# Batch two's v in natural layout through DRAM, and another use of the load buffers

## The chip, the cores and the metric

One core of one Trainium2 chip. The metric is the device time of one execution in microseconds (us). The kernel before takes 226.39 us (median; 226.32 to 226.49). The profile has a span of 224.3 us, since the time also holds some 2 us around it.

## The reference, cut to what matters

```python
batch, n_heads, seq, head_dim = (4, 8, 768, 64);  n_blocks = 8
# P (8 x 8 per head) from sort_net: five rounds of exp and row/column normalisation
k_sorted = einsum('bhij,bhjcd->bhicd', P, k_b)      # blocks of k mixed by P
v_sorted = einsum('bhij,bhjcd->bhicd', P, v_b)      # the same for v
attn = softmax(scale * q_b @ k_sorted^T)            # inside each block of 96
x = attn @ v_sorted                                 # -> (3072 tokens, 512)
h = max(x @ w_in, 0);  out = (h * h) @ w_out        # 512 -> 2048 -> 512
```

## The kernel before

A planner in the kernel lays all work in one order: the attention of one batch fills TensorE between the matrix products of the feed-forward part of the batch before. It fixes the order on TensorE, ScalarE, VectorE and SyncE.

Batches one and two sort v by 128-row matmuls into `vsT`, and turn it by TensorE transposes into `vs`. Batches three and four do it on 32x32 tiles in natural layout, and re-tile the result by a write to DRAM and a read back:

```python
# batches one and two: sort, then turn
for a in range(NA):
    for h in range(2):
        nc.tensor.matmul(out=tp[64*h:64*(h+1), a, :], lhsT=src[:, 2*u.hp+h, D*a:D*(a+1)],
                         rhs=w_all[...], start=True, stop=True)
...
    nc.tensor.transpose(out=vbp[:, n, :], in_=u.vsT[...], identity=ident)

# batches three and four (s_nat): two pairs of heads, 16 matmuls each
nc.tensor.matmul(out=p2[slot][32*c:32*(c+1), h, 0:NA*D], lhsT=w_t[r, ...], rhs=src[r, g, ...],
                 tile_position=(r.start, 32*c))
...
nc.sync.dma_start(out=v_way[b, g]..., in_=vn_r[m]...)     # write
nc.sync.dma_start(out=vb_r[w]..., in_=v_way[b, g]...)     # read back in blocks
```

The attention output of batch two, pairs 0 to 2, goes into `xT` by DMA transposes on SyncE's queue; the feed-forward part of batch two cannot start before all of it is there:

```python
def s_xt(u, due=0, eng=AD):
    if u.b > 1 or u.b == 1 and u.hp < HP - 1:
        def turn(e):
            nc.sync.dma_start_transpose(out=xT[:, u.hp, S*u.b:S*(u.b+1)]..., in_=u.ao...)
```

Loads have two buffers each for q, k and v (`bufs=2`), so batch three takes the first batch's and batch four the second's:

```python
qkv[b] = [ld.tile([128, H, NA * D], BF16, tag=t, name=t) for t in ("qb", "kb", "vb")]
...
def load_late(b):
    for g in range(2):              # first four heads, then last four
        for t in (1, 2, 0):         # k, v, q
            load(b, t, HP * g, HP)
```

The softmax here doesn't subtract the row's maximum and nothing guards it: scores larger than these inputs give would overflow.

Of the kernel before, what the change touches and what calls it, by code (L numbers as in the profile page):

```python
# [128 lines left out]
def kernel(  # L129
# [10 lines left out]
    nc = tc.nc  # L140
# [75 lines left out]

    ksT_r, vsT_r, et_r, vs_r = [], [], [], []
    for n in range(3):
        for r, name, hs in ((ksT_r, "ksT", 2), (vsT_r, "vsT", 2)):
            sT = const.tile([128, hs, HS + 32], BF16, name=f"{name}{n}")  # L220
            nc.vector.memset(sT[:, :, HS:HS + 32], 0.0)
            r.append(sT)
        vs = const.tile([96, NB, 2, 66], BF16, name=f"vs{n}")
        nc.vector.memset(vs[:, :, :, D:D + 1], 1.0)
        vs_r.append(vs)
# [32 lines left out]
    def dma(key, mb, dst_src, deps=()):  # L258
        def issue(e):
            dst, src = dst_src()  # L260
            nc.gpsimd.dma_start(out=dst, in_=src)  # L261
        op = plan.add("POOL", 0.75, issue, deps)
        landed[key] = plan.add("DMA", mb / 0.39, lambda e: None, [op, landed.get("last")])
        landed["last"] = landed[key]

    readers = {b: [] for b in range(B)}

    def alloc_qkv(b):
        if b not in qkv:
            qkv[b] = [ld.tile([128, H, NA * D], BF16, tag=t, name=t) for t in ("qb", "kb", "vb")]  # L270

    def load(b, t, h0, n, p=slice(0, 128)):
        def dst_src():
            alloc_qkv(b)
            if b > 1 and t:
                return (qkv[b][t].rearrange("p (g h) x -> p g (h x)", h=HP)[:, h0 // HP, :],
                        kv_t[t][b, :, h0 // HP, :])
            return qkv[b][t][p, h0:h0 + n, :], (q_r, k_r, v_r)[t][b, p, h0:h0 + n, :]
        dma((b, t, h0, p.start), 1.57 * n / H * (p.stop - p.start) / 128, dst_src,
            readers[b - 2] + [x_done[b - 1, x, 0] for x in range(HP)] if b > 1 else [])  # L280

    def load_w_in(g):
        f = slice(d_ff // 4 * g, d_ff // 4 * (g + 1))
# [7 lines left out]
    mask = const.tile([128, C0], BF16)  # L291
    mask_t = const.tile([128, 4], BF16)

    def make_mask(e):

        src, w = ident, 64
        while w >= 4:
            dst = {C0: mask, 4: mask_t}.get(w) or const.tile([128, w], BF16, name=f"fold{w}")
            nc.gpsimd.tensor_tensor(out=dst, in0=src[:, 0:w], in1=src[:, w:2 * w], op=ALU.add)
            src, w = dst, w // 2  # L300

    for g in range(HP):
        load(0, 1, 2 * g, 2)
# [3 lines left out]
    load_w_in(0)  # L307
    for g in range(1, 4):
        load_w_in(g)
    for g in range(4):  # L310
        t = slice(NT // 4 * g, NT // 4 * (g + 1))
        dma(("w_out", g), 1.05, lambda t=t: (w_out_bf[:, t, :], w_out_r[:, t, :]))
    for g in range(2):
        for t in (2, 1, 0):
            load(1, t, HP * g, HP)


    rs = const.tile([NH, NB], FP32)
# [69 lines left out]
    def build_w(h0, n, src, dep):  # L388
        def fn(e):
            s = tiles["pt_01"] if src is None else src  # L390
            nc.vector.tensor_tensor(
                out=w_all[:, h0:h0 + n, :, :],
                in0=mask[:, None, None, :].to_broadcast([128, n, NB, C0]),
                in1=s[:, :, h0:h0 + n].rearrange("p i h -> p h i")[:, :, :, None]
                .to_broadcast([128, n, NB, C0]),
                op=ALU.mult)
        op = plan.add("DVE", 0.15 + 0.134 * n, fn, [dep])
        for h in range(h0, h0 + n):
            built[h] = op
        return op  # L400
# [94 lines left out]
    def s_sort(u, t, due=0, early=False, eng=AD):  # L495

        st = {}

        def mm(e):
            src = qkv[u.b][t]  # L500
            if early:
                tp = psf.tile([128, 512], FP32, tag="pf", name="tp")
                tp = tp[:, 0:NA * u.ni * C0].rearrange("p (a x) -> p a x", a=NA)
            else:
                tp = (p2[s2].rearrange("p b x -> p (b x)")[:, 0:NA * u.ni * C0]
                      .rearrange("p (a x) -> p a x", a=NA))
            st["p"] = tp
            for a in range(NA):
                for h in range(2):
                    nc.tensor.matmul(  # L510
                        out=tp[64 * h:64 * (h + 1), a, :],
                        lhsT=src[:, 2 * u.hp + h, D * a:D * (a + 1)],
                        rhs=w_all[:, H * u.b + 2 * u.hp + h, u.i0:u.i0 + u.ni, :]
                        .rearrange("p i c -> p (i c)"),
                        start=True, stop=True)

        def ev(e):
            h0 = u.halves[0]
            copy(e, (u.ksT if t == 1 else u.vsT)[:, h0:h0 + len(u.halves), 0:HS]
                 .rearrange("p h (x a) -> p h x a", a=NA),  # L520
                 st["p"].rearrange("p a (h x) -> p h x a", x=NQ * C0))

        h0 = 2 * u.hp
        dep = landed[u.b, t, h0 if u.b == 0 else HP * (h0 // HP), 0]
        ring = rf if early else r2
        s2, old = ring.take()
        pe = plan.add("PE", 0.336 if u.full else 0.2, mm,
                      [dep, built[H * u.b + h0], built[H * u.b + h0 + 1]] + old, due, mode="col")
        readers[u.b].append(pe)
        op = one_of(eng, cost_f(NA * C0 * u.ni), ev, [pe] + u.old)  # L530
        ring.use(s2, pe, op)
        return op

    def s_sc(u, due=0):
# [3 lines left out]
        for hf in u.halves:  # L538
# [4 lines left out]
            def mm(e, hf=hf, st=st, slot=slot):  # L543
# [4 lines left out]
                for n in range(NQ):  # L548
                    for h in range(2):
                        nc.tensor.matmul(  # L550
                            out=scp[:, h, BLK * n:BLK * (n + 1)],
                            lhsT=(u.ksT[64 * h:64 * (h + 1), hf, BLK * n:BLK * n + 128]
                                  if u.b < 2 else
                                  kx_r[u.kx][64 * h:64 * (h + 1), NQ * hf + n::NB]),
                            rhs=(qT[64 * h:64 * (h + 1), NQ * hf + n, :] if u.b < 2 else
                                 qT[64 * h:64 * (h + 1), :, C0 * (NQ * hf + n):
                                    C0 * (NQ * hf + n + 1)]),
                            start=True, stop=True)
# [31 lines left out]
    def s_vt(u, due=0, eng=AD):  # L590
# [3 lines left out]
        def mm(e):  # L594
            st["p"] = vbp = ps1.tile([128, u.ni, 128], BF16, tag="p1", name="vbp")
            for n in range(u.ni):
                i = u.i0 + n
                nc.tensor.transpose(  # L598
                    out=vbp[:, n, :],
                    in_=u.vsT[:, i // NQ, BLK * (i % NQ):BLK * (i % NQ) + 128],  # L600
                    identity=ident)

        def ev(e):
# [13 lines left out]
    def s_nat(b, g, t, due):  # L617
# [4 lines left out]
        for hp in (2 * g, 2 * g + 1):  # L622
# [3 lines left out]

            def mm(e, hp=hp, slot=slot):
                src = qkv[b][t].rearrange("p (g h) x -> p g (h x)", h=HP)
                for h in range(2):
                    r = slice(32 * (2 * (hp % 2) + h), 32 * (2 * (hp % 2) + h + 1))  # L630
                    for c in range(4):
                        nc.tensor.matmul(  # L632
                            out=p2[slot][32 * c:32 * (c + 1), h, 0:NA * D],
                            lhsT=w_t[r, HP // 2 * b + g, :, :].rearrange("p c i -> p (c i)"),
                            rhs=src[r, g, NA * D * c:NA * D * (c + 1)],
                            start=True, stop=True, tile_position=(r.start, 32 * c))

# [25 lines left out]
                out=vb_r[w].rearrange("p i h x -> p (i h x)"),  # L663
                in_=v_way[b, g].rearrange("a (c i) x -> (a c) (i x)", i=NB))

        wr = plan.add("SP", 0.33, write, evs + [loaded(b)])
        there = plan.add("WAY", 2.0, lambda e: None, [wr])
        rd = plan.add("SP", 0.33, read, [there] + oldw)
        back = plan.add("WAY", 2.0, lambda e: None, [rd])
        rvn.use(m, *evs, there)  # L670
        rvb.use(w, back)
        v_blk[b, g] = w, back

    def loaded(b):
        return [landed[b, t, HP, 0] for t in (0,)][0]

    def s_turn(b, hp):

# [35 lines left out]

    def s_av(u, due=0):
        nao, olda = rao.take()
        if u.b > 1:
            w, u.vs_op = v_blk[u.b, u.hp // 2]
        u.norms = []
        for hf in u.halves:  # L720
# [4 lines left out]
            def mm(e, hf=hf, st=st, slot=slot):  # L725
# [3 lines left out]
                for n in range(NQ):  # L729
                    for h in range(2):  # L730
                        nc.tensor.matmul(  # L731
                            out=oup[:, h, 66 * n:66 * n + D + 1],
                            lhsT=et_r[u.et[hf]][:, h, BLK * n:BLK * n + 128],
                            rhs=(u.vs[:, NQ * hf + n, h, 0:D + 1] if u.b < 2 else
                                 vb_r[w][:, NQ * hf + n, 2 * (u.hp % 2) + h, 0:D + 1]),
                            start=True, stop=True)

# [13 lines left out]
            op = plan.add("DVE", 0.9, norm, [pe])  # L751
            r2.use(s2, pe, op)
            ret.use(u.et[hf], pe)
            if u.b < 2:
                rks.use(u.n, pe)
            else:
                rvb.use(w, pe)
# [179 lines left out]
    def lay(b, halves, c0, c1):  # L937
        step, gap = (c1 - c0) / (HP + 0.9), (c1 - c0 - 13) / (HP - 1)
        for hp in range(HP):
# [3 lines left out]
            def open_(due, b=b, hp=hp, box=box):  # L943
# [2 lines left out]
                if b == 1:  # L946
                    build_w(H * b + 2 * hp, 2, pt, kops[b - 1, hp])
                u.k_op = kops[b, hp] = s_sort(u, 1, due)
                u.v_op = s_sort(u, 2, due)

            for f, s in ((0.0, open_),
                         (0.35, lambda due, box=box: s_sc(box["u"], due)),
                         (0.5, lambda due, box=box: s_vt(box["u"], due)),
                         (0.75, lambda due, box=box: s_av(box["u"], due)),
                         (1.2, lambda due, box=box: s_xt(box["u"], due))):
                todo.append((c + step * f, len(todo), s, b))
# [1 line left out]
    def lay_late(b, c0):  # L958

        todo.append((c0, len(todo), lambda due: load_late(b), 0))  # L960
        if b == 2:
            todo.append((c0, len(todo), build_wt, 0))
        for g in range(2):
            for t in (1, 2):
                todo.append((c0 + 9 + 9 * g, len(todo),
# [12 lines left out]
            todo.append((c + 3, len(todo), lambda due, box=box: s_xt(box["u"], due), b))  # L978

    def load_late(b):  # L980
        for g in range(2):
            for t in (1, 2, 0):
                load(b, t, HP * g, HP)

    lay(0, (1,), 0, n_up)
    lay(1, (0, 1), n_up, 2 * n_up)
    lay_late(2, 2 * n_up)
    lay_late(3, 4 * n_up)
    for due, _, stage, b in sorted(todo, key=lambda x: x[:2]):
        stage(int(due))  # L990
# [43 lines left out]
```

## Time and profile before

| | before |
|---|---|
| time, span | 226.39 us, 224.3 us |
| TensorE busy | 97% of the span |
| TensorE waits after 22 us | none listed |
| feed-forward of batch two begins | 82.6 us |
| batch two's DMA transposes of xT | issued from 56.5 to 70.5 us, landing 3.0 to 7.1 us later |

In the time views, a line is start, length, engine, source line, operation, output<-input, shapes and count; a bracket gives the idle time before it and what ended it. In the list of waits, the numbers are us in total, times, and the longest. "To landing" is the time from a transfer's issue to its last byte. Of the names, `p` is a product in PSUM (the memory that TensorE writes to), `hp` and `op` are the up- and the down-projection's, `ao` is the attention output and `xT` the same turned, `kn` the sorted k and `kx` the same turned; an eviction is the copy of a product out of PSUM by VectorE or ScalarE. The prediction below shows the views of the kernel before on which it rests.

### The profile page before, as it was taken

What the parts mean: (1) busy time and instruction counts of PE and PEld (TensorE: products, weight loads), DVE (VectorE), ACT (ScalarE), POOL (GpSimd) and SP (SyncE); (2) the same over time, 40 slices, a digit from 0 to 9 for tenths busy, and PEclk for the clock granted to TensorE, in tenths of its full rate; (3) what the DMA queues carried; (4) which work ended last, traced back from release to release, by engine and by line L of the source; (5) the groups of instructions that cost most, each with busy time, mean ns of one, the idle gap of its engine ahead of it and who ended that gap; (6) DMA issues with size and microseconds to landing.
All of it is one profiled execution on the core that took longest, in us unless ns stands there. A gap on an engine that the chain in (4) does not pass through costs nothing.

```text
span 224.3 us, 5245 instructions
## 1 busy us (share of the span) xinstructions
PE 216.6 (97%) x2130; PEld 122.9 (55%) x2145; DVE 105.7 (47%) x297; ACT 122.1 (54%) x253; POOL 26.4 (12%) x46
## 2 busy tenths in 40 slices
PE   7898999999999999999999999999999999999994
PEld 2476665556665645545665455445665465446553
DVE  6777777317666416640666127523664045005400
ACT  4665776228885328734775248535774177137521
POOL 7962332200004200000000000000000000000000
PEclk9999999999999999999999999999999999999999
DMA  5999999999953996499941320899522410110012
GB/s 66 201 202 208 207 206 205 203 227 245 210 65 27 191 239 145 115 216 201 220 38 35 85 94 0 164 225 254 110 37 43 122 47 1 50 57 37 0 50 94
DMA packets 42744, 28.83 MB, mean 129 GB/s; under 512 B 22752, under 2 KB 38368, under 8 KB 42720
## 3 DMA queue, kind: packets, MB, share of 16 engines
q0 software_dynamic: 13888, 13.63, 37.1%
q1 hardware_dynamic: 28832, 14.86, 29.7%
q8 instruction: 17, 0.28, 0.5%
q14 instruction: 7, 0.06, 0.1%
HBM read 28.89 MB, written 7.91 MB: 164 GB/s over the span
## 4 chain that ended last, share of the span: by engine, by line
PE 92%; DMA 2%; DVE 2%; ACT 1%; issue 1%; ACTq 0%; POOLq 0%
PE hp L810 37%; PE op L838 35%; PE p L550 4%; PE p L731 3%; DMA qb<-in_q_dram 2%; PE p L510 2%; PE qtp L461 2%; PE vbp L598 2%; PE op L872 2%; PE p L350 1%; PE p L632 1%; PE xtp L779 1%; PE tp L510 1%; DVE ao L742 1%; ACT h L818 0%
## 5 line engine op out<-in xcount | busy, mean ns | idle before, releaser
L810 PE MATMUL hp<-xT,w_in_bf 128*128 128x384 bf16 x512 | 91.0, 326 | 0.0
L838 PE MATMUL op<-w_out_bf,h 128*128 128x512 bf16 x353 | 82.6, 379 | 0.8
L818 ACT ACTIVATE h<-hp 128x384 bf16<-128x384 f32 x128 | 62.0, 495 | 23.5 <-PE hp L810 20.0
L821 DVE TENSOR_TENSOR h<-h 128x384 bf16<-128x384 bf16 x128 | 44.5, 355 | 56.3 <-ACT h L818 55.5
L810 PEld LDWEIGHTS <-w_in_bf 128*128 128x128 bf16 x512 | 47.0, 98 | 30.0 <-issue 0.7
L838 PEld LDWEIGHTS <-h 128*128 128x128 bf16 x368 | 34.7, 98 | 39.4 <-issue 0.7
L192 ACT COPY ob<-op 128x512 f32<-128x512 f32 (+1 forms) x25 | 14.2, 569 | 56.0 <-PE op L838 50.6
L742 DVE TENSOR_TENSOR ao<-p,rec 96x512 bf16<-96x512 f32 x32 | 22.0, 687 | 1.4 <-DVE rec L741 0.3
L582 ACT ACTIVATE et<-p 96x384 bf16<-96x384 f32 x48 | 19.4, 491 | 2.4 <-PE p L550 2.4
L741 DVE RECIPROCAL rec<-p 96x8 f32<-96x8 f32 x32 | 6.4, 199 | 13.6 <-PE p L731 13.3
L731 PEld LDWEIGHTS <-et 96*128 96x128 bf16 x256 | 10.6, 97 | 2.9
L261 POOL DMA_DIRECT2D qb<-in_q_dram x8 | 6.0, 754 | 32.5 <-PE qtp L461 24.4
L350 PE MATMUL p<-ones 128*128 128x512 bf16 (+1 forms) x36 | 8.8, 360 | 1.1 <-DVE ones L213 1.1
L194 DVE COPY vs<-vbp 96x512 bf16<-96x512 bf16 (+1 forms) x12 | 6.1, 508 | 7.1 <-PE vbp L598 6.9
L573 ACT ACTIVATE et<-p 96x768 bf16<-96x768 f32 x8 | 6.3, 802 | 2.1 <-PE p L550 2.0
L261 POOL DMA_DIRECT2D kb<-in_k_dram x10 | 6.6, 659 | 6.6 <-DMA w_in_bf<-in_moe_w_in_dram 2.2
L261 POOL DMA_DIRECT2D vb<-in_v_dram x10 | 6.6, 660 | 6.4 <-DMA w_in_bf<-in_moe_w_in_dram 3.6
L192 ACT CAST ksT<-p 128x768 bf16<-128x768 f32 (+1 forms) x7 | 4.6, 662 | 3.3 <-PE p L510 3.3
L550 PEld LDWEIGHTS <-kx 64*128 64x128 bf16 x128 | 4.6, 155 | 2.8 <-issue 2.8
L731 PE MATMUL p<-vs,et 96*128 96x65 bf16 x128 | 6.0, 193 | 0.0
L461 PE MATMUL qtp<-ident,qb 64*64 64x64 bf16 (+1 forms) x144 | 4.7, 204 | 1.3 <-DMA qb<-in_q_dram 1.3
L461 PEld LDWEIGHTS <-qb 64*64 64x64 bf16 (+1 forms) x144 | 3.5, 109 | 4.5 <-DMA qb<-in_q_dram 2.3
(78 smaller groups left out, 129.3 us busy)
## 6 DMA issues: line engine op xcount, KB each, us to landing
out_dram<-ob SPq DMA_DIRECT2D x23, 256.0 KB, 2.8
qb<-in_q_dram POOLq DMA_DIRECT2D x8, 384.0 KB, 15.7
vb<-in_v_dram POOLq DMA_DIRECT2D x6, 384.0 KB, 17.1
kb<-in_k_dram POOLq DMA_DIRECT2D x6, 384.0 KB, 17.1
w_in_bf<-in_moe_w_in_dram POOLq DMA_DIRECT2D x4, 512.0 KB, 12.5
w_out_bf<-in_moe_w_out_dram POOLq DMA_DIRECT2D x4, 512.0 KB, 18.0
v_way<-vn SPq DMA_DIRECT2D x4, 396.0 KB, 4.1
vblk<-v_way SPq DMA_DIRECT2D x4, 396.0 KB, 3.9
```

The costliest lines, as they stand in the source:

```text
L192: nc.scalar.copy(out=out, in_=in_)
L261: nc.gpsimd.dma_start(out=dst, in_=src)
L350: nc.tensor.matmul(out=out, lhsT=ones, rhs=rhs, start=True, stop=True)
L461: nc.tensor.transpose(out=t["p"][64 * h:64 * (h + 1), a, :], in_=qb[p0:p1, 2 * hp + h, D * a:D * (a + 1)], identity=ident[p0:p1, p0:p1])
L550: nc.tensor.matmul(out=scp[:, h, BLK * n:BLK * (n + 1)], lhsT=(u.ksT[64 * h:64 * (h + 1), hf, BLK * n:BLK * n + 128] if u.b < 2 else kx_r[ ...
L582: nc.scalar.activation(out=et[:, h, 0:HS].rearrange("p (n c a) -> p n c a", c=C0, a=NA), in_=st["p"][0:96, h, 0:HS].rearrange("p (n a c) - ...
L731: nc.tensor.matmul(out=oup[:, h, 66 * n:66 * n + D + 1], lhsT=et_r[u.et[hf]][:, h, BLK * n:BLK * n + 128], rhs=(u.vs[:, NQ * hf + n, h, 0: ...
L742: nc.vector.tensor_tensor(out=u.ao[:, n0:n0 + NQ, :, :].rearrange("p n e d -> p e n d"), in0=ov[:, :, :, 0:D], in1=rec[:, :, :, None].to_b ...
L810: nc.tensor.matmul(out=t["hp", nt][:, 0:HS], lhsT=w_in_bf[:, kc, 128 * nt:128 * (nt + 1)], rhs=xT[:, kc, t0:t0 + HS], start=(kc == 0), sto ...
L818: nc.scalar.activation(out=t["h1", nt], in_=t["hp", nt][:, 0:HS], func=AF.Relu)
L821: nc.vector.tensor_tensor(out=t["h2"][:, nt, :], in0=t["h1", nt], in1=t["h1", nt], op=ALU.mult)
L838: nc.tensor.matmul(out=t["op", mt], lhsT=t["h2"][:, nt, 128 * mt:128 * (mt + 1)], rhs=w_out_bf[:, nt, :], start=(nt == 0), stop=(nt == NT ...
```

## The change

Batch two's v goes the way that batches three and four go: 32 matmuls on 32x32 tiles in place of 48 sorting matmuls and 32 transposes on TensorE, and four transfers through DRAM more. Half of that v is loaded ahead of w_out. Batch three takes the second batch's buffers, batch four the first's, and late loads take the last four heads first. The cuts leave out a second mask for batch two's order of k, the flat `ksT` and `vsT`, new estimates of transfer times and a new `loaded` in the planner (the load behind which late work is planned), and renamed indices.

```diff
 def alloc_qkv(b):
     if b not in qkv:
-        qkv[b] = [ld.tile([128, H, NA * D], BF16, tag=t, name=t) for t in ("qb", "kb", "vb")]
+        m = (b + 1) // 2 % 2
+        qkv[b] = [ld.tile([128, H, NA * D], BF16, tag=f"{t}{m}", name=t, bufs=1)
+                  for t in ("qb", "kb", "vb")]
...
-            readers[b - 2] + [x_done[b - 1, x, 0] for x in range(HP)] if b > 1 else [])
+            readers[(0, 0, 1, 0)[b]] + [x_done[b - 1, x, 0] for x in range(HP)] if b > 1 else [])
...
+    load(1, 2, 0, HP)                 # ahead of w_out
...
-    for g in range(2):
-        for t in (2, 1, 0):
-            load(1, t, HP * g, HP)
+    for t, g in ((2, 1), (1, 0), (0, 0), (1, 1), (0, 1)):
+        load(1, t, HP * g, HP)
...
-                u.v_op = s_sort(u, 2, due)
+                if b == 0:
+                    u.v_op = s_sort(u, 2, due)
+            if b == 1 and hp % 2 == 0:
+                todo.append((14 + 2 * hp, len(todo),
+                             lambda due, g=hp // 2: s_nat(1, g, 2, due), b))
...
-        for g in range(2):
+        for g in (1, 0):
             for t in (1, 2, 0):
                 load(b, t, HP * g, HP)
...
+    todo.append((8, len(todo), build_wt, 0))
-    lay_late(2, 2 * n_up)
+    lay_late(2, 2 * n_up + 3)
```

More of the change, by code (lines that the diff above doesn't have):

```diff
@@ L218 @@
     for n in range(3):
-        for r, name, hs in ((ksT_r, "ksT", 2), (vsT_r, "vsT", 2)):
-            sT = const.tile([128, hs, HS + 32], BF16, name=f"{name}{n}")
-            nc.vector.memset(sT[:, :, HS:HS + 32], 0.0)
+        for r, name in ((ksT_r, "ksT"), (vsT_r, "vsT")):
+            sT = const.tile([128, S + 32], BF16, name=f"{name}{n}")
+            for x in (HS, S):
+                nc.vector.memset(sT[:, x:x + 32], 0.0)
             r.append(sT)
@@ L262, in dma @@
         op = plan.add("POOL", 0.75, issue, deps)
-        landed[key] = plan.add("DMA", mb / 0.39, lambda e: None, [op, landed.get("last")])
+        landed[key] = plan.add("DMA", mb / (0.39 if key[0] == 0 else 0.43), lambda e: None, [op, landed.get("last")])
         landed["last"] = landed[key]
@@ L274, in dst_src @@
             alloc_qkv(b)
-            if b > 1 and t:
+            if b > 1 and t or b == 1 and t == 2:
                 return (qkv[b][t].rearrange("p (g h) x -> p g (h x)", h=HP)[:, h0 // HP, :],
@@ L292 @@
     mask_t = const.tile([128, 4], BF16)
+    mask_1 = const.tile([128, C0], BF16)
     def make_mask(e):
@@ L300, in make_mask @@
             src, w = dst, w // 2
+        nc.gpsimd.tensor_copy(out=mask_1.rearrange("p (z y) -> p z y", y=4),
+                              in_=mask.rearrange("p (y z) -> p z y", z=4))
     for g in range(HP):
@@ L392, in fn @@
                 out=w_all[:, h0:h0 + n, :, :],
-                in0=mask[:, None, None, :].to_broadcast([128, n, NB, C0]),
+                in0=(mask if h0 < H else mask_1)[:, None, None, :]
+                .to_broadcast([128, n, NB, C0]),
                 in1=s[:, :, h0:h0 + n].rearrange("p i h -> p h i")[:, :, :, None]
@@ L517, in ev @@
         def ev(e):
-            h0 = u.halves[0]
-            copy(e, (u.ksT if t == 1 else u.vsT)[:, h0:h0 + len(u.halves), 0:HS]
-                 .rearrange("p h (x a) -> p h x a", a=NA),
-                 st["p"].rearrange("p a (h x) -> p h x a", x=NQ * C0))
+            dst = u.ksT if t == 1 else u.vsT
+            if u.b == 0:
+                copy(e, dst[:, BLK * u.i0:BLK * (u.i0 + u.ni)]
+                     .rearrange("p (x a) -> p x a", a=NA), st["p"].rearrange("p a x -> p x a"))
+            else:
+                copy(e, dst[:, 0:S].rearrange("p (n a x) -> p n a x", a=NA, x=C0),
+                     st["p"].rearrange("p a (n x) -> p n a x", x=C0))
         h0 = 2 * u.hp
@@ L551, in mm @@
                             out=scp[:, h, BLK * n:BLK * (n + 1)],
-                            lhsT=(u.ksT[64 * h:64 * (h + 1), hf, BLK * n:BLK * n + 128]
+                            lhsT=(u.ksT[64 * h:64 * (h + 1), HS * hf + BLK * n:HS * hf + BLK * n + 128]
                                   if u.b < 2 else
@@ L599, in mm @@
                     out=vbp[:, n, :],
-                    in_=u.vsT[:, i // NQ, BLK * (i % NQ):BLK * (i % NQ) + 128],
+                    in_=u.vsT[:, BLK * i:BLK * i + 128],
                     identity=ident)
@@ L628, in mm @@
                 src = qkv[b][t].rearrange("p (g h) x -> p g (h x)", h=HP)
+                w = w_t[:, HP // 2 * b + g, :, :].rearrange("p c i -> p (c i)")
                 for h in range(2):
@@ L633, in mm @@
                             out=p2[slot][32 * c:32 * (c + 1), h, 0:NA * D],
-                            lhsT=w_t[r, HP // 2 * b + g, :, :].rearrange("p c i -> p (c i)"),
+                            lhsT=w[r, :],
                             rhs=src[r, g, NA * D * c:NA * D * (c + 1)],
@@ L664, in read @@
                 in_=v_way[b, g].rearrange("a (c i) x -> (a c) (i x)", i=NB))
-        wr = plan.add("SP", 0.33, write, evs + [loaded(b)])
-        there = plan.add("WAY", 2.0, lambda e: None, [wr])
+        wr = plan.add("SP", 0.33, write, evs + ([loaded(b)] if b > 1 else []))
+        slow = 6.0 if b == 1 else 2.0
+        there = plan.add("WAY", slow, lambda e: None, [wr])
         rd = plan.add("SP", 0.33, read, [there] + oldw)
-        back = plan.add("WAY", 2.0, lambda e: None, [rd])
+        back = plan.add("WAY", slow, lambda e: None, [rd])
         rvn.use(m, *evs, there)
@@ L674, in loaded @@
     def loaded(b):
-        return [landed[b, t, HP, 0] for t in (0,)][0]
+        return landed[b, 0, 0, 0]
     def s_turn(b, hp):
@@ L716, in s_av @@
         nao, olda = rao.take()
-        if u.b > 1:
+        if u.b > 0:
             w, u.vs_op = v_blk[u.b, u.hp // 2]
@@ L733, in mm @@
                             lhsT=et_r[u.et[hf]][:, h, BLK * n:BLK * n + 128],
-                            rhs=(u.vs[:, NQ * hf + n, h, 0:D + 1] if u.b < 2 else
+                            rhs=(u.vs[:, NQ * hf + n, h, 0:D + 1] if u.b < 1 else
                                  vb_r[w][:, NQ * hf + n, 2 * (u.hp % 2) + h, 0:D + 1]),
@@ L753, in s_av @@
             ret.use(u.et[hf], pe)
-            if u.b < 2:
+            if u.b < 1:
                 rks.use(u.n, pe)
@@ L948, in open_ @@
                 u.k_op = kops[b, hp] = s_sort(u, 1, due)
-                u.v_op = s_sort(u, 2, due)
+                if b == 0:
[3 more added lines that the diff above has]
+                             lambda due, g=hp // 2: s_nat(1, g, 2, due), b))
             for f, s in ((0.0, open_),
                          (0.35, lambda due, box=box: s_sc(box["u"], due)),
-                         (0.5, lambda due, box=box: s_vt(box["u"], due)),
+                         (0.5, lambda due, box=box: b == 0 and s_vt(box["u"], due)),
                          (0.75, lambda due, box=box: s_av(box["u"], due)),
@@ L960, in lay_late @@
         todo.append((c0, len(todo), lambda due: load_late(b), 0))
-        if b == 2:
-            todo.append((c0, len(todo), build_wt, 0))
         for g in range(2):
```

## The prediction

> **What bounds the kernel now.** I read the page's busy table and slices first, then the chain that ended last, then what TensorE waited for, then TensorE in order of time in the second batch, and last the DMA queues and issues.
>
> From the page:
> ```profile
> PE 216.6 (97%) x2130; PEld 122.9 (55%) x2145; DVE 105.7 (47%) x297; ACT 122.1 (54%) x253; POOL 26.4 (12%) x46
> ...
> PE   7898999999999999999999999999999999999994
> ...
> PE 92%; DMA 2%; DVE 2%; ACT 1%; issue 1%; ACTq 0%; POOLq 0%
> ```
> TensorE is busy from the second slice to the last but one. Busy alone proves little, since pipelined matmuls overlap in the records; the chain does prove it: 92% of the span is TensorE followed by TensorE. VectorE and ScalarE are at half. What TensorE waited for in the whole run:
> ```profile
> PE qtp L461 <- DMA qb<-in_q_dram: 1.3, 1, 1.3
> PE p L350 <- DVE ones L213: 1.1, 1, 1.1
> PE xtp L779 <- DVE vs L194: 0.6, 1, 0.6
> ...
> ```
> With two more of 0.3 and 0.2 us that is 3.5 us, all before 22 us in the time view, where the change alters nothing on TensorE. From 22 us on, the end is set by the sum of what TensorE has to stream. So each block of matmuls that goes is worth its own time there, unless something new makes TensorE wait.
>
> TensorE in order of time, at the start of the second batch (start, length, what):
> ```profile
> 49.39 0.53 PE L461 MATMUL qtp<-ident,qb 128*64 128x128 bf16 x12
> 49.75 0.50 PE L510 MATMUL p<-w_all,kb 128*64 128x128 bf16 x12
> 50.08 0.50 PE L510 MATMUL p<-w_all,vb 128*64 128x128 bf16 x12
> 50.52 1.47 PE L810 MATMUL hp<-xT,w_in_bf 128*128 128x384 bf16 x8
> 51.92 0.51 PE L550 MATMUL p<-qT,ksT 64*128 64x96 bf16 x16
> 52.37 0.62 PE L598 MATMUL vbp<-ident,vsT 128*128 128x128 bf16 x8
> 52.83 1.46 PE L810 MATMUL hp<-xT,w_in_bf 128*128 128x384 bf16 x8
> ...
> 56.93 0.53 PE L510 MATMUL p<-w_all,vb 128*64 128x128 bf16 x12
> 57.39 0.82 PE L810 MATMUL hp<-xT,w_in_bf 128*128 128x384 bf16 x4
> 58.15 0.71 PE L550 MATMUL p<-qT,ksT 64*128 64x96 bf16 x16
> 58.79 0.82 PE L810 MATMUL hp<-xT,w_in_bf 128*128 128x384 bf16 x4
> 59.45 0.61 PE L598 MATMUL vbp<-ident,vsT 128*128 128x128 bf16 x8
> 59.90 1.46 PE L810 MATMUL hp<-xT,w_in_bf 128*128 128x384 bf16 x8
> ```
> The lengths overlap, so I read costs as start to start. The sort of v (L510, vb) is 50.52-50.08 = 0.44 us and its transpose back (L598) 52.83-52.37 = 0.46. Entering a tiled block from the full array costs too: eight hp matmuls before a full-array block take 1.30 (52.83 to 54.13), before a tiled block 1.40 (50.52 to 51.92), so 0.10. Leaving is in the tiled block's own time: L550 before hp takes 0.64 (58.15 to 58.79), before the transposes 0.45.
>
> **What the Trainium skill says.** "TensorEngine Tiling (Array Packing)", Key Properties: changing the tiling mode drains TensorE. The trace agrees: 0.10 us on entry and 0.1 to 0.2 on leaving. "TensorE: Matmul & The Clock Gate", Measured speedup vs the span model: tiles run together, a pack lasts about one matmul plus 4 ns for each further tile. The third batch already does it this way:
> ```profile
> 88.57 0.38 PE L632 MATMUL p<-kb,w_t 32*32 32x384 bf16 x16
> 88.88 1.47 PE L810 MATMUL hp<-xT,w_in_bf 128*128 128x384 bf16 x8
> ```
> One matmul there is 0.33 us and 15 x 4 ns make 0.39; the trace has 0.38. "DMA: Bandwidth & Descriptors", Issuing engines are not separate DMA queues: transfers issued by SyncE and GpSimd share the 16 DMA engines and interleave. The trace agrees: a 256 KB store takes 2.8 us as a median of all, but 5.6 in the window from 38 to 55 us, where loads keep every DMA engine busy.
>
> **The change part by part.** From the order of instructions in the two built programs, after the first up-projection.
>
> Removed: for four pairs of heads of batch two, 12 sorting matmuls and 8 transposes, 80 matmuls. Hand-summed by start to start, with the order that each pair gets:
> - Pair 0: the v sort follows the k sort without a change of mode, so 0.33 (49.75 to 50.08 is one such block); L550 and the transposes take 0.91 together and L550 alone will take 0.64, so 0.27. Sum 0.60.
> - Pair 1: sort 0.46 and transpose 0.45, less 0.10 because the k sort no longer follows the q transposes and the switch remains. Sum 0.81.
> - Pair 2: sort 0.46, its entry 0.10, transpose 0.45. Sum 1.01.
> - Pair 3: sort 0.33 to 0.46, transposes 0.27 as in pair 0. Sum about 0.67.
> Together 3.1 us.
>
> Added: 32 matmuls on 32x32 tiles, as two blocks of 16 in the first batch's stage. Each costs 0.31 (88.57 to 88.88) plus 0.10 of entry, 0.41; one block of the third batch took 0.53 (96.96 to 97.49), since it waited for one of the two PSUM buffers that a block needs both of. The first new block comes right behind scores whose exponential still holds a buffer, so I take 0.41 to 0.63 each: 0.8 to 1.3 us.
>
> Moved: the small build of w_t goes from 82.45 us to the first batch's stage, alone between other work in both: 0. The third batch starts its attention 12 matmuls of up-projection later: the sum stays the same. VectorE and ScalarE lose 8 evictions of second-batch v and gain 4; neither sets the end. Six more memsets of about 0.05 us lie ahead of the wait for the first exponential on VectorE, where it was idle for 0.53 us; one small copy on GpSimd is ahead of loads that already queue behind each other. Both 0.
>
> Sum: -3.1 +0.8 to +1.3, that is -1.8 to -2.3, middle -2.1 us.
>
> **The rivals.** (1) *The way through DRAM comes late.* v leaves TensorE at about 36 us and 42.5 us; the attention product of pair 0 moves to about 55.5 (54.13 plus 0.8 to 1.3 for the new blocks, less 0.6, plus 0.65 for four hp matmuls now ahead of it). In between lie the eviction (about 1 us) and two transfers:
> ```profile
> v_way<-vn SPq DMA_DIRECT2D x4, 396.0 KB, 4.1
> vblk<-v_way SPq DMA_DIRECT2D x4, 396.0 KB, 3.9
> ```
> These are medians in a quieter stretch. If loads double them as they do the stores, 8 us each: out at 37.5, written by 45.5, read by about 53.5, allowing for the second write that stands ahead of the read on SyncE. Two us are left. If they took 10 us each, TensorE would wait up to 2 us and the gain would be gone. Pair 2, which uses the second half, has over 8 us to spare.
>
> (2) *Loads come too late.* Putting half of batch two's v ahead of w_out delays it. DMA moves about 205 GB/s there, so 384 KB is 1.9 us. The last quarter of w_out was issued at about 17 us and landed up to 20.5 us later, by 37.6; now 39.5. TensorE asks for it at about 41 (41.09 before). The other half of v lands at about 41.3, and its block comes at about 42. Tight by 1 us; a miss costs under 1 us. In the other direction, these v loads have rows four times as long, which may make them shorter.
>
> (3) *The third batch starves.* Its loads now wait for the second batch's buffers instead of the first's, so they cannot start before the last q transposes of batch two, at about 68 us:
> ```profile
> 70.57 0.75 POOL L261 DMA_DIRECT2D qb<-in_q_dram  x1 [24.43 <-PE qtp L461]
> ```
> In the old kernel that wait belongs to batch four; six such loads landed 10 to 13 us after it. So the third batch would be there at 80 to 82 us, and its first block comes at about 88. Batch four's loads follow at once, to about 93 us, and take bandwidth from the third batch's transposes; those have some 6 us before the first scores at about 104. I expect no wait, only less spare time. If it failed, it would cost 2 to 5 us.
>
> For rival outcomes: all hidden gives 224.3; one partial wait 224.8 to 226; starvation of batch three 226 to 230.
>
> **Range and chances.** 226.39 - 2.1 = 224.3; for small waits in the crowded first stage I add 0.1 and say 224.4. The range, 223.7 to 225.5, holds the hand sum's full spread below, and one wait of about a microsecond above. Faster by over 2% needs 4.5 us, more than everything that is removed: 2%. Slower by over 2% needs starvation of several us: 2%. Within 2%: 96%.
>
> **What would show it.** TensorE should have 48 matmuls fewer, no vb sort and no L598-type transposes between 50 and 78 us, and two new blocks on 32x32 tiles near 36 and 42 us of 0.3 to 0.55 us each. The up-projection after batch two's attention should begin 2 us earlier than 82.61. The list of waits of TensorE should show no new entry over 0.5 us on vblk, w_out or batch two's v. The transfers of v_way should take 5 to 8 us while loads run. GpSimd should sit idle till about 68 us and then issue 12 loads in a row. I am wrong if TensorE waits for vblk near 55 us, if the loads of batch three land after 88 us, or if the blocks saved turn out to have filled slack that the evictions impose anyway, so that hp matmuls stretch in their place.

## The result, and the profile after

The changed kernel is not faster. Its four first executions took 227.24, 227.52, 234.95 and 237.53 us (median 231.24); the kernel before stayed at 226.3 to 226.5. By the two fast runs alone the ratio is 1.0043 (95% interval 1.0019 to 1.0068). Ratios here are the mean time of one kernel's fast runs over that of the other's fast runs of the same rounds, so not quite the ratio of the medians. A run over 1.5% above the fastest of its kernel counts as slow. The first experiment shows that these slow runs are this kernel's own; the profile below is of the run of 227.52 us, a fast one.

The page of the changed kernel:
```profile
PE 216.2 (96%) x2097; PEld 120.5 (54%) x2097; DVE 102.6 (46%) x299; ACT 121.2 (54%) x253; POOL 26.1 (12%) x47
...
PE 82%; DMA 8%; DVE 6%; ACT 2%; issue 1%; POOL 0%; DVEq 0%; ACTq 0%
```
TensorE's share of the chain fell from 92% to 82%, and DMA's rose from 2% to 8%. Something other than TensorE sets the end for a stretch. What TensorE waited for, two lines that the kernel before does not have:
```profile
PE hp L824 <- DMA xT<-ao: 1.9, 1, 1.9
...
PE p L645 <- DVE kn L194: 0.8, 1, 0.8
```
TensorE in order of time, first the start of batch two's feed-forward part in the kernel before:
```profile
82.61 6.02 PE L810 MATMUL hp<-xT,w_in_bf 128*128 128x384 bf16 x36
```
In the changed kernel, the two new blocks and the same start:
```profile
35.93 0.66 PE L645 MATMUL p<-vb,w_t 32*32 32x384 bf16 x16
...
42.50 0.38 PE L645 MATMUL p<-vb,w_t 32*32 32x384 bf16 x16
...
80.28 0.49 PE L824 MATMUL hp<-xT,w_in_bf 128*128 128x384 bf16 x2
82.63 7.63 PE L824 MATMUL hp<-xT,w_in_bf 128*128 128x384 bf16 x46 [1.86 <-DMA xT<-ao]
```
TensorE arrives at batch two's feed-forward part at 80.28 us in place of 82.61: the 2.3 us are there. Two matmuls later it stands for 1.86 us. The chain of work in order of time says for what:
```profile
69.05 13.54 DMA xT<-ao
82.59 0.04 issue
82.63 7.63 PE hp L824 x46
```
The third DMA transpose of batch two was issued at 69.05 us and landed 13.5 us later. In the window from 55 to 84 us, the three transposes into xT of the kernel before:
```profile
DMA to landing us min/median/max: 3.0/6.8/7.1
```
and of the changed kernel:
```profile
DMA to landing us min/median/max: 11.9/13.5/15.8
```
The same transfers take two to four times as long. GpSimd in order of time tells what else was going on (the loads from 34 us on that matter):
```profile
34.62 0.74 POOL L262 DMA_DIRECT2D qb<-in_q_dram  x1 [2.04 <-PE xtp L793]
...
50.17 0.53 POOL L262 DMA_DIRECT2D vb<-in_v_dram  x1 [2.78 <-DMA kb<-in_k_dram]
53.04 0.53 POOL L262 DMA_DIRECT2D vb<-in_v_dram  x1 [2.35 <-DMA qb<-in_q_dram]
69.42 0.75 POOL L262 DMA_DIRECT2D qb<-in_q_dram  x1 [15.84 <-PE qtp L470]
```
Eight late loads are issued between 34 and 53 us, and four (q, k, k, q) from 69 us. In the kernel before it was six and six. The first six fill the first batch's buffers, now for batch four. The two more are v loads for batch three: batch two's v is sorted by 43 us now, so its buffer comes free some 26 us before its q and k. The planner does not fix GpSimd's order: there the framework issues a load when the buffer that it fills is free. The DMA queues from 38 to 55 us show the trips of v through DRAM beside them:
```profile
vblk<-v_way SPq DMA_DIRECT2D x2, 396.0 KB, 7.4
...
v_way<-vn SPq DMA_DIRECT2D x1, 396.0 KB, 9.7
```

### The profile page after: what moved, and what is told of

Its sections match the earlier page's. It is cut to its first block, busy times and chain, and to the rows that moved or that the text cites. A ratio compares the mean times of both kernels' runs of the same rounds, so it can differ in the third digit from the quotient of the medians.

```text
span 225.2 us, 5181 instructions
## 1 busy us (share of the span) xinstructions
PE 216.2 (96%) x2097; PEld 120.5 (54%) x2097; DVE 102.6 (46%) x299; ACT 121.2 (54%) x253; POOL 26.1 (12%) x47
## 4 chain that ended last, share of the span: by engine, by line
PE 82%; DMA 8%; DVE 6%; ACT 2%; issue 1%; POOL 0%; DVEq 0%; ACTq 0%
PE hp L824 37%; PE op L852 30%; DMA xT<-ao 6%; PE p L562 4%; PE p L745 3%; DVE ao L756 2%; PE op L886 2%; DMA kx<-kn 1%; PE p L645 1%; PE p L519 1%; PE vbp L610 1%; PE tp L519 1%; PE xtp L793 1%; DVE p_sb L338 1%; DMA p_sb<-in_sort_net_dram 1%
## 5 line engine op out<-in xcount | busy, mean ns | idle before, releaser
L852 PE MATMUL op<-w_out_bf,h 128*128 128x512 bf16 x368 | 83.6, 379 | 0.0
L832 ACT ACTIVATE h<-hp 128x384 bf16<-128x384 f32 x128 | 61.1, 497 | 23.6 <-PE hp L824 18.2
L835 DVE TENSOR_TENSOR h<-h 128x384 bf16<-128x384 bf16 x128 | 44.0, 355 | 65.4 <-ACT h L832 64.6
L192 ACT COPY ob<-op 128x512 f32<-128x512 f32 (+1 forms) x24 | 13.6, 567 | 59.2 <-PE op L852 56.6
L358 PE MATMUL p<-ones 128*128 128x512 bf16 (+1 forms) x36 | 9.6, 388 | 1.1 <-DVE ones L213 1.1
L262 POOL DMA_DIRECT2D qb<-in_q_dram x8 | 6.0, 752 | 24.1 <-PE qtp L470 15.8
L745 PE MATMUL p<-vblk,et 96*128 96x65 bf16 x192 | 8.3, 193 | 0.0
L194 DVE CAST vn<-p 128x768 bf16<-128x768 f32 x6 | 5.7, 956 | 3.3 <-PE p L645 3.3
L192 ACT CAST ksT<-p 128x384 bf16<-128x384 f32 (+1 forms) x7 | 4.3, 614 | 3.3 <-PE p L519 3.3
L194 DVE CAST kn<-p 128x768 bf16<-128x768 f32 x4 | 3.8, 956 | 4.1 <-DMA kx<-kn 2.1
L562 PE MATMUL p<-qT,kx 64*128 64x96 bf16 x128 | 5.6, 227 | 0.0
## 6 DMA issues: line engine op xcount, KB each, us to landing
w_in_bf<-in_moe_w_in_dram POOLq DMA_DIRECT2D x4, 512.0 KB, 11.9
```

The lines of the kernel that those rows point to most:

```text
L192: nc.scalar.copy(out=out, in_=in_)
L194: nc.vector.tensor_copy(out=out, in_=in_)
L262: nc.gpsimd.dma_start(out=dst, in_=src)
L358: nc.tensor.matmul(out=out, lhsT=ones, rhs=rhs, start=True, stop=True)
L562: nc.tensor.matmul(out=scp[:, h, BLK * n:BLK * (n + 1)], lhsT=(u.ksT[64 * h:64 * (h + 1), HS * hf + BLK * n:HS * hf + BLK * n + 128] if u. ...
L745: nc.tensor.matmul(out=oup[:, h, 66 * n:66 * n + D + 1], lhsT=et_r[u.et[hf]][:, h, BLK * n:BLK * n + 128], rhs=(u.vs[:, NQ * hf + n, h, 0: ...
```

## The experiments

Theory A: loads that now start early keep the DMA engines full while batch two's transposes run. Rival B: the trips through DRAM do. Rival C: the exchange of buffers does. All runs below gave correct results. There are ten runs.

### 1. The changed kernel again

No edit.

> The changed kernel once more, for the spread of its times. If the slow executions (two of four, at a granted clock of 0.98) belong to this kernel, one to three of six are slow again; if they were chance of that one chip, none is. Fast runs: 227.2 to 227.6 us, ratio to the kernel before 1.003 to 1.006, with TensorE waiting 1 to 3 us for the DMA transposes of xT near 80 us.

Measured: 229.96 to 239.23 us in six runs, median 233.58; ratio of the runs counted as fast 1.0187 (1.0148 to 1.0226). Eleven runs of the kernel before on the same chip lie between 226.34 and 226.83. So the scatter belongs to this kernel: all ten executions so far, 227.24 to 239.23 us, lie above all of the kernel before. Three of the six count as slow here, and the verdict by rule is "unclear". The time was worse than expected: no run came below 229.9. The profiled run (232.41 us) has this wait:
```profile
PE hp L824 <- DMA xT<-ao: 4.5, 1, 4.5
```
and in stretches of 4 us (busy us and count of each engine, then the granted TensorE clock, the DMA share and GB/s):
```profile
80.00:84.00 4.00, 0.81 (x5) 0.29 (x3) 0.00 (x0) 0.59 (x1) 0.00 (x0) 0.88 1.38 96
84.00:88.00 4.00, 2.72 (x9) 1.28 (x9) 0.44 (x2) 0.98 (x2) 0.00 (x0) 0.50 1.07 244
88.00:92.00 4.00, 4.00 (x20) 2.14 (x19) 1.53 (x5) 2.02 (x5) 0.00 (x0) 0.77 0.75 168
```
The wait is paid twice. The granted clock falls to half at about 83.0 us, while TensorE stands, and is back only at about 89.9 us: the 46 up-projection matmuls take 9.88 us in place of 7.63. After the wait of 1.9 us in the first profile the clock stayed at 1.00. This agrees with the Trainium skill, "TensorE: Matmul & The Clock Gate", HAM oscillation: gaps above about 3.4 us bring the clock down; here it had fallen 2.2 us into the gap. The runs of this kernel have mean clocks from 0.978 to 0.993 here, and the two slowest the lowest. Only the profiled runs show where the clock fell; that the other slow runs have the same cause is an inference.

### 2. Batch two's v buffer held until 70 us

```diff
+            if b == 1 and hp == HP - 1:
+                def hold(due, box=box):      # one tiny copy that reads batch two's v late
+                    keep = const.tile([128, 2, 2], BF16, name="keep")
+                    readers[1].append(plan.add("DVE", 0.1, lambda e: nc.vector.tensor_copy(
+                        out=keep, in_=qkv[1][2].rearrange("p (g h) x -> p g (h x)", h=HP)[:, :, 0:2]),
+                        [box["u"].k_op]))
+                todo.append((c + step * 0.1, len(todo), hold, b))
```

> The changed kernel, with one tiny VectorE copy near 70 us that reads batch two's v, so that its buffer comes free with the others and the two v loads that were issued at 50 and 53 us wait until about 70 us. Theory A (those early loads keep the DMA engines full while batch two's xT transposes run): the first two transposes land in 3 to 8 us in place of 12 to 16, TensorE's wait for xT near 80 us goes, 225.0 to 225.6 us. Rival B (the v_way traffic and its place on SyncE's queue delay the transposes): the wait of about 1.9 us stays, 227 us or more. Rival C (six loads at 70 us delay the last transpose as much): the wait stays or grows.

Measured: 225.40 us (225.38 to 225.60, five runs), ratio 0.9949 (0.9936 to 0.9962), clock 1.00. The wait for xT is gone. In the same window:
```profile
DMA to landing us min/median/max: 4.9/7.7/12.4
```
Theory A's time is met, and rivals B and C in their strong form are out: the trips and the exchange are still there. But the first transpose, at 12.4 us, is still much slower than the 3 to 8 that A expected. So the trips cost the transposes something too.

### 3. The third pair turned by TensorE

```diff
-        if u.b > 1 or u.b == 1 and u.hp < HP - 1:
+        if u.b > 1 or u.b == 1 and u.hp < HP - 2:
```

> The changed kernel, with the third pair of batch two turned by TensorE (8 transposes, 0.34 us and about 0.1 more) in place of the last DMA transpose. If the last transpose is what TensorE waited for, the second lands at about 75.6 us and the wait near 80 us goes: 1.9 less, 0.4 more, 225.7 to 226.2 us. If the DMA engines delay something else as well (batch three's last loads, due at about 86 to 88 us), a new wait near 88 to 90 us takes part of it and the time stays above 226.5.

Measured: 225.78 us (225.59 to 226.75), ratio 0.9975 (0.9958 to 0.9992). The wait for the DMA is gone, which confirms that it is the transposes that TensorE stood for. Two of six runs are near 226.7. The two remaining transposes took 17.7 us each; the second, issued near 63.4 us, landed at about 81.1, with TensorE asking at 81.84. It was luck by less than a microsecond, and not the 75.6 us that I had expected. Nor did the slow transposes cost nothing. The profile is of one of the two slower runs (226.61 us), and in it VectorE waits until the first transpose has read its buffer:
```profile
75.76 0.69 DVE L756 TENSOR_TENSOR ao<-p,rec 96x512 bf16<-96x512 f32 x1 [1.30 <-DMA xT<-ao]
```
TensorE stands for 0.9 us behind it, and so asks that much later. Whether this is what sets the two slower runs apart is not shown.

### 4. The kernel before with the exchange of buffers and the load order alone

```diff
-        qkv[b] = [ld.tile(..., tag=t, name=t) for t in ("qb", "kb", "vb")]
+        m = (b + 1) // 2 % 2
+        qkv[b] = [ld.tile(..., tag=f"{t}{m}", name=t, bufs=1) for t in ("qb", "kb", "vb")]
...
-        for g in range(2):
+        for g in (1, 0):
```

> The kernel before, with only the new use of buffers and order of the late loads. Its v stays as it was, so all of batch two's buffers come free together at about 70 us. Theory A and rival B both: the same six loads early and six late as before, only for the other batch, so no wait for xT; 226.2 to 226.7 us. If the exchange of buffers itself costs (batch three's loads late, at about 83 us), a wait near 88 us: 227 us or more.

Measured: 226.40 us, ratio 0.9994 (0.9982 to 1.0006); landings of 3.0, 6.9 and 7.0 us. By itself the exchange does nothing. (The cut leaves out `readers` and `loaded`, which follow as in the change.)

### 5. The changed kernel without the exchange

```diff
-            m = (b + 1) // 2 % 2
+            m = b % 2
...
-            readers[(0, 0, 1, 0)[b]] + ...
+            readers[b - 2] + ...
```

> The changed kernel with the old use of buffers (batch three into the first batch's, batch four into the second's). v in natural layout still frees its buffer at about 43 us. If the early release of v is the cause (theory A), it is now batch four's two v loads that are issued near 50 us: the wait for xT near 80 us stays at 1.5 to 5 us and the times scatter as in the changed kernel, 227 to 239 us. If the exchange of buffers is a part of the cause, the wait goes and the time is 225 to 226.5 us.

Measured: 235.81 to 238.10 us in four runs, ratio 1.0470 (1.0427 to 1.0514).
```profile
PE hp L824 <- DMA xT<-ao: 7.8, 1, 7.8
```
The wait is longer than I had allowed for, and all four runs lie in the upper part of the expected range. From 84 to 88 us the clock was 0.70, and 0.50 from 88 to 92. Rival C is out: without the exchange the wait stays. Whether it is worse is not shown: run 1 was on another chip, and its six times, 229.96 to 239.23 us, take in these four. The loads were issued at the same times within about 0.6 us.

### 6. All 12 late loads held until 69 us

As in 2, and the first batch's three buffers held by three more tiny copies:
```diff
+                    for t in range(3):
+                        keep0 = const.tile([128, 2, 2], BF16, name=f"keep{t}")
+                        readers[0].append(plan.add("DVE", 0.1, ..., [box["u"].k_op]))   # reads qkv[0][t]
```

> As the run with v held back, with the first batch's buffers held until about 70 us as well: all 12 late loads start at about 69 us, which is the schedule that the prediction took for granted. With no backlog of loads from about 47 us, the first two xT transposes land in about 3 us each; the third, in front of 12 loads, in 5 to 8 us. If batch three's loads go first, they land by about 81 us, in time: 225.2 to 225.8 us. If batch four's share the queue with them, a wait for batch three's k at about 88 us: 226.5 to 229 us.

Measured: 232.32 us (231.76 to 233.39), ratio 1.0260 (1.0231 to 1.0290). The transposes into xT land in 2.7, 3.0 and 4.6 us, as expected. But the wait comes elsewhere:
```profile
97.20 0.35 PE L645 MATMUL p<-vb,w_t 32*32 32x384 bf16 x8
102.32 0.52 PE L645 MATMUL p<-vb,w_t 32*32 32x384 bf16 x8 [4.77 <-DVE kn L194]
```
Batch three's loads were in time; its own q and k transposes were not, behind batch four's loads. VectorE stood from 92.6 to 101 us for a q transpose, and the eviction that TensorE needed stands behind that copy. VectorE's line for it is
```profile
101.04 0.36 DVE L709 COPY qi<-qb 128x768 bf16<-128x768 bf16 x1 [8.44 <-DMA qT<-qi]
```
The clock fell at the end of this wait too (mean 0.77 from 100 to 104 us). Both of my expectations missed it: the time, and the place.

### 7. v held, and a fourth buffer for the sorted k

On top of 2:
```diff
-    kn_r = [... for n in range(3)]
+    kn_r = [... for n in range(4)]
-    rkx, rkn, rqi = Ring(3), Ring(3), Ring(2)
+    rkx, rkn, rqi = Ring(3), Ring(4), Ring(2)
```

> As the run with v held back, with a fourth buffer for batch three's and four's sorted k in natural layout, so that the eviction at about 144 us need not wait for a DMA transpose of an older one. That wait of 0.77 us on TensorE is gone: 225.4 less 0.5 to 0.8, 224.6 to 224.9 us. If the eviction waits for something else too (the PSUM buffer, the transposes' order), the time stays at 225.3 to 225.5.

Measured: 224.47 us (224.47 to 224.60), ratio 0.9908 (0.9892 to 0.9925). The wait near 144 us is gone; the list of waits has only those of the first 22 us. With run 9 this is the fastest kernel; the two do not differ clear of noise.

### 8. The kernel before with the trips through DRAM as dead traffic

```diff
+    def way(due, g):
+        w, oldw = rvb.take()
+        u = plan.add("DVE", 0.5, lambda e: nc.vector.memset(vn_r[g][:, :, :, 0:D], 0.0), [...])  # mended
+        wr = plan.add("SP", 0.33, ... dma_start(out=v_way[1, g]..., in_=vn_r[g]...), [u])
+        there = plan.add("WAY", 6.0, lambda e: None, [wr])
+        rd = plan.add("SP", 0.33, ... dma_start(out=vb_r[w]..., in_=v_way[1, g]...), [there] + oldw)
...
+    todo.append((13, len(todo), lambda due: way(due, 0), 0))
+    todo.append((19, len(todo), lambda due: way(due, 1), 0))
```

> The kernel before, with the trips of v through DRAM added as dead traffic in batch two's time (two writes of 396 KB at about 36 and 43 us, two reads back; nothing uses them). If the trips alone delay the transposes (rival B): the first xT transpose lands in 12 to 16 us, the last in over 11, and TensorE waits near 82 us: over 227.5 us. If it needs the early v loads (theory A): the first transpose lands in 9 to 12.5 us in place of 7.1, as with v held back, the last in 5 to 8, no wait: 226.3 to 226.9 us.

Measured: 226.74 us, ratio 1.0007 (0.9993 to 1.0022), no new wait.
```profile
DMA to landing us min/median/max: 6.5/6.8/13.1
```
The trips alone delay the first transpose by 6 us and the last by nothing. (The writes were issued at 31.7 and about 37 us, 5 us earlier than intended.) Rival B alone is out; run 2, with the trips at their true times, says the same.

### 9. v held, and the late loads in the old order

On top of 2:
```diff
-        for g in (1, 0):
+        for g in range(2):
...
-        return landed[b, 0, 0, 0]
+        return landed[b, 0, HP, 0]
```

> As the run with v held back (225.40 us), with the late loads in the old order, first heads first. In the built program this moves one thing on TensorE: batch four's first k block comes after 36 up-projection matmuls as in the kernel before, not 44, so it lies 1.3 us further from the second k block, whose eviction needs the same buffers. If the new load order made the wait of 0.77 us near 144 us, it goes: 224.4 to 224.8 us. If that wait comes from something else (the transposes being slower), 225.2 to 225.5.

Measured: 224.49 us (224.46 to 224.66), ratio 0.9915 (0.9900 to 0.9930).
```profile
134.90 0.38 PE L645 MATMUL p<-kb,w_t 32*32 32x384 bf16 x16
...
142.01 0.38 PE L645 MATMUL p<-kb,w_t 32*32 32x384 bf16 x16
142.32 1.04 PE L852 MATMUL op<-w_out_bf,h 128*128 128x512 bf16 x4
143.29 0.60 PE L645 MATMUL p<-vb,w_t 32*32 32x384 bf16 x16
```
The two k blocks are 7.1 us apart again, where the run with the new order has 5.8 (136.00 to 141.81 us), and the wait is gone. So the second wait needs the new order of loads: the planner believes that batch four's first heads land later (in the trace they landed long before), and puts the block off by eight matmuls. The following eviction then needs a k buffer whose DMA transpose is still on its way, in run 2:
```profile
143.20 0.96 DVE L194 CAST kn<-p 128x768 bf16<-128x768 f32 x1 [2.13 <-DMA kx<-kn]
```
The order alone does not make it: run 4 has it too, with the blocks 7.1 us apart and no wait. What else of the change is needed was not tested. A fourth buffer (run 7) or the old order cures it equally.

### 10. The kernel before with early v loads alone

A third v buffer for batch four, and five instead of six q buffers to make room. The streams of TensorE, ScalarE, VectorE and SyncE are the same as before.
```diff
-        qkv[b] = [ld.tile(..., tag=t, name=t) for t in ("qb", "kb", "vb")]
+        qkv[b] = [(ld3 if b == 3 and t == "vb" else ld).tile(..., tag=t, name=t) for t in ("qb", "kb", "vb")]
```

> The kernel before, with a third v buffer for batch four (and five instead of six q buffers to make room): the streams of TensorE, ScalarE, VectorE and SyncE stay the same, but two more v loads run early and q, k, k, q are left for 70 us, as in the changed kernel, without the trips through DRAM. Loads alone: two loads are 786 KB or about 3.5 us more backlog, so the first xT transpose lands in 10 to 13 us in place of 7.1, the second in 3 to 9, the third in 6 to 10, and no wait: 226.3 to 226.8 us. If the loads alone make the changed kernel's wait (trips not needed), the third lands over 11 us after its issue and the time is over 227.5.

Measured: 226.64 us, ratio 1.0009 (0.9993 to 1.0026), no new wait.
```profile
DMA to landing us min/median/max: 5.9/7.1/12.2
```
Early loads alone do not make the wait either. Theory A as I first put it falls: it takes both. In runs 8 and 10 the third transpose landed by 77.0 and 77.6 us, so TensorE would not have waited for it at the changed kernel's 80.6 us either.

## Why the prediction was wrong

**What held.** TensorE is the bound after 22 us, and what it loses in blocks it gains in time. The predicted sum of -2.1 us (-1.8 to -2.3) is what the change brings once no new wait is in the way: the medians of run 7 say 224.47 - 226.54 = -2.07 us, of run 9 224.49 - 226.39 = -1.90. The new blocks cost 0.59 (35.93 to 36.52) and 0.32 us; with 0.10 of entry that is 0.69 and 0.42, where I had 0.41 to 0.63 each. Rival 1 came as near as feared: the writes took 9.6 and 9.7 us, not the 5 to 8 forecast, and the first trip was read back by about 55.3 us (47.12 plus the 8.2 of that read) and used at 55.70. Of the two us that were to be left, 0.4 were. Rival 2 did not happen: TensorE has no wait for w_out.

**The step that failed first** is in rival 3 and in what would show it: "GpSimd should sit idle till about 68 us and then issue 12 loads in a row". GpSimd was idle from 53 to 69 us and issued four. I took the loads to go in the planner's order. They go as buffers come free, and the trace of the kernel before showed it: six late loads at 36 to 46 us, long before the planner's dependence on batch two's attention could have held. By the diff, the first batch's buffers, now batch four's, are free first, and batch two's v next.

**The path that I left out** is the DMA transposes of batch two. This is the step that cost the time. The prediction has no wait there; TensorE stood for 1.86 us (4.5 and 7.8 us in runs 1 and 5) at the up-projection that I named as a check. The kernel before gave the numbers: the third was issued at 70.5 us and landed 6.8 us later, at 77.3, for a use at 82.6. That is 5.3 us to spare, of which the change itself takes 2.3. I weighed the load of the DMA engines against every other transfer, and not against this one.

How long these transposes take, by what the DMA engines carry beside them (landing times of the first, second and third, us):

| | no early v loads | early v loads |
|---|---|---|
| no trips | 7.1, 3.0, 6.8 (before) | 12.2, 5.9, 7.1 (run 10) |
| trips | 13.1, 6.8, 6.5 (run 8); 12.4, 7.7, 4.9 (run 2) | 15.8, 11.9, 13.5 (after); 17.7, 18.7, 21.2 (run 5) |

Each cause alone costs the first transpose 5 to 6 us and the last next to nothing. The last is the only one with a narrow margin. Both together cost the last one 6.7 us or more. The traces fit one reading: with one cause alone, the first two transposes are through by about 70 or 71 us (57.9 + 12.4 = 70.3 and 63.4 + 7.7 = 71.1 in run 2), when the third transpose and the last loads have just started. With both they are not (57.9 + 15.8 = 73.7 and 63.4 + 11.9 = 75.3 in the changed kernel), and three transposes and four loads run together. DMA then moves far less: 75 GB/s from 76 to 80 us against 238 in run 2, though its engines count as busier (1.81 against 1.07). It does not take three transposes: in run 3, with two, it is 68 GB/s. This overlap as the cause of the fall in throughput is argued from these stretches and not tested by itself.

**"Moved: ... the sum stays the same"** was wrong by 0.77 us. The block was moved nearer to one that shares its buffers, and run 9 shows that it takes the new load order for it.

**The sum in the changed kernel's trace**: 2.33 earlier at 80.28 us, 1.86 of wait for xT, 0.77 for the k eviction, which leaves 0.30 longer than before; its span is 0.9 longer. So from 80 us on it has a surplus of some 0.6 us beyond the waits. Run 2, without the first wait, has one of about 0.46 us beyond the 0.77 (223.2 - 80.28 = 142.92 against 224.3 - 82.61 = 141.69). It is in pieces of 0.1 to 0.2 us that I did not trace.

**The fallback was wrong as well.** Run 6 is the schedule that I took for granted. I had written of it "I expect no wait, only less spare time". It takes 232.3 us, since batch four's loads starve batch three's transposes.

**The scatter** was not in the prediction at all. In three traces a wait (4.5, 4.8 and 7.8 us) took TensorE's clock to half: it fell 2.2, 4.6 and 3.1 us into the wait and was back 4.6, 3.1 and 5.6 us after its end. The wait of 1.9 us left it at 1.00. What makes the transposes land 13.5 us after issue in one run and over 16 in another stays open.

## What to carry to other kernels

Ask of a freed buffer when its next load will start, and which transfers that load will then run beside; the order in which a program lists its loads may not be the order in which they are issued. For each transfer that a saturated engine will wait for, write down its slack in the old trace before giving the DMA queues more to do. A gain on the bounding engine is lost twice if it turns into one long wait, as the clock went down with each wait of 4.5 us or more here; a tiny late read that holds a buffer was enough to keep the gain.

## What the Trainium skill lacked or had wrong

- "DMA: Bandwidth & Descriptors", DMA Transpose (X-bar): nothing on how much longer a transpose takes beside other traffic. Here the same transposes of 96x1024 elements landed after 2.7 to 3.0 us with little beside them (the first two of run 6), after 5 to 13 with trips or early v loads, and after 12 to 21 with both, while the total rate fell to 65 to 75 GB/s from 76 to 80 us, against 229 in the kernel before.
- The same page, Issuing engines are not separate DMA queues: that all transfers interleave on the same 16 engines agrees. What it lacks is the size of the effect: a write of 396 KB took 9.7 us beside loads, against 4.1 as the median of all six.
- "TensorE: Matmul & The Clock Gate", HAM oscillation: the gap of about 3.4 us agrees so far as tested (1.9 us kept the clock, 4.5, 4.8 and 7.8 lost it; none lies between, and in run 1 the clock fell after 2.2). It prices gaps for a kernel that stalls at every tile, and not a single gap in one that is otherwise full: in run 1, 4.5 us of wait cost 2.25 us more through the clock in the next 46 matmuls (9.88 against 7.63 us).
